# Attention with a borrowed PSUM bank for the row maxima, and the burst of products with v moved to the end of its head step

## The chip, the core and the metric

The kernel runs on one core of one Trainium2 chip. The core's engines are TensorE (PE, matrix products; its weight loads are listed apart as PEld), VectorE (DVE), ScalarE (ACT), GpSimd (POOL) and SyncE (SP, which issues most of the DMAs). Each engine works through its own queue in order. Products are written to PSUM, eight banks of 128 partitions by 512 float32 numbers; DVE and ACT read them there. The metric is the device time of one execution in microseconds, as the median of several runs; one more execution was profiled, and all rows of the trace come from that one.

## The reference

Two independent computations are laid side by side. The second is a spectral filter, a 2-D real FFT of a 2048 x 576 array, a product with complex weights, and the inverse transform. The change does not touch it. The first, cut to what matters here:

```python
B, S, D = 1, 2048, 576;  H = 32; Dh = 18; N = 4; L = 512
q, k, v = x @ wq, x @ wk, x @ wv              # split into 32 heads and 4 segments
for s in range(N):
    logits = q_s @ k_s^T * scale + mask       # causal within the segment
    p = softmax(logits);  a_dot = p @ v_s
    pq = phi(q_s);  a_mem = (pq @ M) / (pq @ z + 1e-6)
    o = g * a_mem + (1 - g) * a_dot           # g = sigmoid(beta) by head
    M += phi(k_s)^T @ v_s;  z += sum(phi(k_s))
out = o @ wo
```

So there are 4 segments x 32 heads = 128 score matrices of 512 x 512, of which the lower triangle counts. The softmax subtracts the maximum of each row.

## The kernel before

The program runs in stages: the forward FFT with the loads of weights, the projections to q, k and v, the inverse FFT with the first maxima, and then the attention, which is where the change lies. q, k and v are stored in DRAM and read back in stacks of 8 heads (`Qs`, `Ks`, and `vs` for v). A stack's rows 0 to 107 carry three-way bfloat16 splits of the 18 values of a head; rows 108 and 109 of `Qs` hold the row maxima, so that the second product of scores comes out with the maxima already subtracted.

**The loop.** `attention` loops over head steps t = 0 to 132, one head per step; four heads (a quad, k = t // 4, hh = t % 4) share a tile. The order is written out by hand: the order in which the source issues instructions is that of each engine's queue. One step interleaves several lines of work, most of them Python generators that `steps` advances:

- `s1(t+11)` is the first pass for the head eleven steps ahead. It forms the scores in parts, two for an even head, three for an odd one (the third part holds a block of each head of the pair). Each `part` takes a PSUM bank `s1`, of which the pool `ps1` has three, makes one or two products on PE (L687), each of 128 to 512 columns, and has DVE add the mask and take the row maxima (L691) into `mg`. As t+11 is odd when t is even, the step with three parts has even t.
- `s2(t)` is the second pass: scores transposed (L723, L727 and L728, in odd steps also L733 for the pair), and exp on ACT (L724, L729, L734) into the tiles `P`. I call these three tiles p0, p1 and p2. They have three banks, tag `s2`. After the fourth head of a quad POOL clears the upper triangle (`sel`, L736); the rest of the selections come one step later (`s.rest`).
- `pv` is the product of P with v (L760), float32, four heads side by side in 32-column strips of the array. It comes in bursts of eight calls, which the trace shows as 16 products with as many weight loads, at odd t: t % 4 = 1 opens the bank `pv` of the quad before, t % 4 = 3 completes it, and `pv_out` copies it to `U` on ACT (from t = 117 on, on DVE). From there it goes to DRAM (`u_dmas`).
- `mpath(k+2)` carries the maxima of a quad from columns to rows: POOL casts (L703, L704), in the next step (hh = 1) PE transposes (L707, into a bank `s1`), ACT copies (L710), and two steps later ACT issues the DMA into rows 108 and 109 of `Qs` (L713).
- The background list `bg`, advanced by `run_bg` at a rate of 1.0 to 1.35 calls a step, holds the set-up of the output weights, the denominators of the memory part (`den`, L811), the mixing of memory and attention (`mixed`, with `combine` L884 and `mem1` L835 and L841) and the output projection of the segment before (`oproj`, L908). Its products take the one bank `post`, through the function `post`; from t = 117 on they take `s1` banks, as the maxima are then all done. `late_setup`, the first entry, takes no bank.
- `lane` holds the chains of reciprocals (`recip`, L785 and L786 on DVE).

PSUM during the loop: `s1` three banks, `s2` three, `pv` one, `post` one.

Within one step the order is: first part of the maxima, p0, background left over, second part, p1, the burst (odd t), background, third part (even t), transposition (t % 4 = 1), p2 (odd t), the copy of the transposition.

After the loop the last output projection runs (`last_proj`, L937), with small products (L917) between.

Of the kernel before, what the change touches and what calls it, by code (L numbers as in the profile page):

```python
# [5 lines left out]
F32=mybir.dt.float32; F32R=mybir.dt.float32r  # L6
# [403 lines left out]
class ATT:  # L410
# [268 lines left out]
    def s1(s,t):  # L679

        nc=s.nc; k,hh=divmod(t,4); n,qd=divmod(k,2); h=4*qd+hh
        Q,K=s.Qs[n%3],s.Ks[n%4]; tp=s.sm
        assert (n,0) in s.loaded and (n,1) in s.loaded,(t,n)
        if hh==0: s.mg[k]=tp.tile([128,4,4],F32,name="mg")
        def part(*J):
            p=s.ps1.tile([128,512],F32,name="s1",tag="s1")
            for o,i,e in J: nc.tensor.matmul(p[:,o:o+128*i+128],Q[:108,h+e,128*i:128*i+128],K[:108,h+e,:128*(i+1)],start=True,stop=True)  # L687
            for o,i,e in J:
                w=128*(i+1); b=max(256,w-128*e)
                junk=tp.tile([128,b],BF,name=f"junk{b}",bufs=1)  # L690
                nc.vector.tensor_tensor_reduce(out=junk[:,:w],in0=p[:,o:o+w],in1=s.mask[:,512-w:],scale=1.0,scalar=-3.0e38,  # L691
                    op0=OP.add,op1=OP.max,accum_out=s.mg[k][:,hh+e,i:i+1])
        part((0,2,0),(384,0,0))
        yield
        part((0,3,0))
        yield
        if hh%2: part((0,1,-1),(256,1,0))
        yield
# [247 lines left out]
    def begin(s,sm,sp,ps1):  # L946
        s.late=[]; s.now=-1
        s.sm,s.sp,s.ps1=sm,sp,ps1
        s.mh=sm.tile([128,8,16],BF,name="mh",bufs=1); s.nc.gpsimd.memset(s.mh,0.0)
        s.mg={};s.P={};s.vs={};s.rc={};s.am={};s.pq={};s.ux={};s.rate=1.2;s.potag=s.rest=None  # L950
    def prologue(s):

        nc,io=s.nc,s.io
        yield
        s.load_v(0)
        q=s.stack_dmas(1,0)+s.stack_dmas(1,1)+s.stack_dmas(2,0)+s.stack_dmas(2,1)+[lambda: s.load_v(1)]+s.stack_dmas(3,1)
        for i in range(2): yield
        i=0
        for t in range(11):
            for _ in s.s1(t):  # L960
                for _ in range(1+(i%24==0)):
                    if q: q.pop(0)()
                i+=1
                yield
            if 2<=t<6: nc.gpsimd.dma_start(s.Ks[t-2][108:110].rearrange("p h c -> p (h c)"),io["neg1"])
            if t in (3,7): m=s.mpath(t//4); next(m)
            if t in (4,8): next(m); next(m,None)
        assert not q
# [3 lines left out]
    def attention(s,tp,ps):  # L972
        nc=s.nc; s.tp,s.ps,s.psm,s.mtag=tp,ps,s.ps1,"s1"
        s.homes()
        def steps(gen,i):
            for _ in range(i):
                try: next(gen)
                except StopIteration: return
        m=None
        q=[]  # L980
        qu=[]
        bg=[s.late_setup(tp)]
        state=dict(acc=0.0)
        def run_bg(rate):
            state["acc"]+=rate
            if state["acc"]>=1:
                state["acc"]-=1
                while bg:
                    try: next(bg[0]); break
                    except StopIteration: bg.pop(0)  # L990
        lane=[]
        for t in range(133):
            k,hh=divmod(t,4); n,qd=divmod(k,2); g=k//8
            if hh==0 and qd==0:
                if 0<n<14: q+=s.stack_dmas(n+2,0)
                if 0<n<13: q+=s.stack_dmas(n+3,1)
                if n+2<16: q.insert(6,lambda n=n: s.load_v(n+2))
            st=t%32
            if t in (18,21,24,27,30): s.pq_load(1,ORD[(18,21,24,27,30).index(t)])
            if t==34: bg.append(s.den(1,lane))  # L1000
            if st==8 and g>0:
                def ln(g=g):
                    r=s.recip(s.rD[g-1],s.rrD[g-1],s.g1,False,"rr",2)
                    for i in range(8):
                        if 2<i<6: s.ux_load(g-1,ORD[i-3])
                        next(r); yield
                    yield from r
                    bg.append(s.mixed(g))
                    o=s.oproj(g-1)
                    if g<3: bg.append(itertools.islice(o,4)); bg.append(s.den(g+1,lane))  # L1010
                    bg.append(o)
                lane.append(ln())
            if t==125: lane.append(s.recip(s.rD[3],s.rrD[3],s.g1,False,"rr"))
            a=s.s1(t+11) if t+11<128 else iter(())
            b=s.s2(t) if t<128 else iter(())
            for _ in range(3 if t%8==0 else 1):
                if q: q.pop(0)()
            if qu: qu.pop(0)()
            steps(a,1)
            steps(b,1)  # L1020
            run_bg(0)
            steps(a,1)
            steps(b,1)
            if 4<=t-1<132: s.pv((t-5)//4,(t-5)%4)
            run_bg(s.rate)
            steps(a,1)
            if hh==1 and m is not None: steps(m,1)
            steps(b,1)
            if hh==1 and m is not None: steps(m,1)
            if hh==0 and k+2<32: m=s.mpath(k+2); next(m)  # L1030
            if hh==0 and s.rest: s.rest(); s.rest=None
            if t>=7 and t%4==3:
                s.pv_out((t-7)//4)
                if t%8==3:
                    u=s.u_dmas((t-11)//8)
                    if t<124: s.later(1,lambda u=u: qu.extend(u))
                    else: qu+=u
            for l in list(lane):
                try: next(l)
                except StopIteration: lane.remove(l)  # L1040
            if qu: qu.pop(0)()
            s.due(t)
        assert not q
        s.potag="s2"; s.last_parts()
        if qu: qu.pop(0)()
        b=s.recip(s.rD[3],s.rrD[0],s.g1,False,"rd"); next(b)
        for u in range(3): s.ux_load(3,u)
        while qu: qu.pop(0)()
        i=0
        while bg or i<10:  # L1050
            for l in list(lane):
                try: next(l)
                except StopIteration: lane.remove(l)
            run_bg(1.0)
            i+=1
            s.due(132+i)
            if i in (3,8,10): s.last_tile((3,8,10).index(i),"rr")
            if i==3: s.ux_load(3,3)
            if i==5: next(b); next(b); next(b)
            if i in (6,7): next(b)  # L1060
            if i==7: s.ux_load(3,4)
        assert not lane
        s.due(999)
        for _ in b: pass
        s.last_low()
        for t in range(3):
            for u in range(7):
                s.last_proj(u,t)
                if t==2 and u==3: s.last_low()
                if t==2 and u in (1,4): s.last_tile(3 if u==1 else 4,"rd")  # L1070
        s.last_low()
        for u in range(7): s.last_proj(u,3)
        o=[s.tp.tile([128,4,512],F32,name=f"P{i}").rearrange("p a b -> p (a b)") for i in range(2)]
        o=[o[tb//3][:,576*(tb%3):576*(tb%3)+576] for tb in range(4)]
        nc=s.nc
        for u in range(8):
            if u==6:
                for t in range(4): s.last_proj(7,t)
            tb,hf=divmod(u,2); s.last_proj(u,4); c=slice(288*hf,288*hf+288) if u>5 else slice(0,576)
            (nc.vector.tensor_copy if hf else nc.scalar.copy)(o[tb][:,288*hf:288*hf+288],s.acc[u])  # L1080
            if hf or u>5: nc.sync.dma_start(s.io["ya"][1536+128*tb:1664+128*tb,c],o[tb][:,c])
# [108 lines left out]
```

## Time and profile before

| | |
|---|---|
| median of 3 runs | 684.14 us (683.86 to 684.6) |
| profiled execution | 683.95 us |
| its span, first to last instruction | 682.2 us |
| mean granted TensorE clock | 0.999 |
| instructions | 14101 |
| first product of the second pass (L723) | at 347.6 us |
| last product of the first pass (L687) | at 617.9 us |
| last burst of products with v (L760) | at 645.0 us |

How to read the rows: a row of the timeline has the start in us, the time it took, the engine, the line, the operation, what it writes <- what it reads, the partitions and elements, how many instructions are merged into it, and in brackets the idle time of the engine before it and what ended it. A matmul's end is modelled and includes its way through the array, so two that follow each other overlap in the rows; the distance of their starts is what PE spends on one. A row of the chain that ended last has start, length, engine, tile, line and count. A row of a table of windows has the window, its length, and the busy time of PE, PEld, DVE, ACT and POOL with the number of instructions, then clock, DMA share and GB/s; where the view was asked for one engine it has only that one. A row of a line's group has the count, the durations in ns (least, median, most) and the first and the last start.

### The profile page before, as it was taken

To read this page: it belongs to the slowest core of one execution; us is meant where nothing else is said; L and a number is where in the kernel's file an instruction comes from. 1 tells how busy PE (TensorE), PEld (TensorE's weight loads), DVE (VectorE), ACT (ScalarE), POOL (GpSimd) and SP (SyncE) were. 2 spreads that over 40 slices of the span, in tenths; PEclk is the share of its full clock that TensorE was granted. 3 is DMA by queue.
4 is the path that set the end of the run, shared out by engine and by line. 5 is a ranking of instruction groups with operands and counts; after the bars stand their busy time and mean duration, and the time that the engine had idled before them with its cause. 6 is when DMAs were issued, how large, how long until landed. Compare 5 with 4: busy or idle time off the path is not lost.

```text
span 682.2 us, 14101 instructions
## 1 busy us (share of the span) xinstructions
PE 669.0 (98%) x4776; PEld 487.0 (71%) x4776; DVE 541.0 (79%) x1509; ACT 433.5 (64%) x900; POOL 193.0 (28%) x392
## 2 busy tenths in 40 slices
PE   9999999999999999999989999999999999999997
PEld 5999779879879879999954444444566445663497
DVE  5998989889789779598778888998766888667543
ACT  4876795585585384544358877777756777656521
POOL 2111000100200102556416433445323663135410
PEclk9999999999999999999999999999999999999999
DMA  9896476596387679699336765776646576423152
GB/s 338 301 311 186 137 198 200 151 300 203 113 240 222 178 211 319 196 284 272 110 121 176 207 185 151 204 205 174 173 139 188 155 186 167 125 87 92 29 170 78
DMA packets 76034, 127.57 MB, mean 187 GB/s; under 512 B 12813, under 2 KB 44203, under 8 KB 72371
## 3 DMA queue, kind: packets, MB, share of 16 engines
q1 hardware_dynamic: 69310, 110.67, 55.7%
q0 software_dynamic: 5632, 15.76, 8.0%
q8 instruction: 37, 0.61, 0.4%
q10 hardware_dynamic: 1020, 0.25, 0.2%
q14 instruction: 35, 0.28, 0.1%
HBM read 81.78 MB, written 43.92 MB: 184 GB/s over the span
## 4 chain that ended last, share of the span: by engine, by line
PE 84%; DVE 5%; DMA 4%; ACT 3%; issue 2%; POOL 1%; SPq 0%; ACTq 0%; DVEq 0%; POOLq 0%
PE pj L487 15%; PE pv L760 11%; PE s L687 11%; PE pjv L487 8%; PE po L908 5%; PE i L331 4%; PE i L320 4%; PE f L145 4%; PE c L166 4%; PE s L723 3%; PE s L727 3%; PE pn L835 2%; PE s L733 2%; PE po L937 2%; PE pm L559 2%
## 5 line engine op out<-in xcount | busy, mean ns | idle before, releaser
L691 DVE CUSTOM_DVE_ANT_0 junk<-s,x 128x384 bf16<-128x384 f32 (+3 forms) x512 | 219.6, 486 | 49.0 <-PE s L687 47.6
L736 POOL TENSOR_SCALAR_AFFINE_SELECT P<-P 128x512 f32<-128x512 f32 (+2 forms) x135 | 80.3, 617 | 61.3 <-ACT P L724 58.0
L760 PE MATMUL pv<-P,vs 128*32 128x512 f32 (+3 forms) x1024 | 82.2, 439 | 0.5 <-POOL P L736 0.4
L724 ACT ACTIVATE P<-s 128x512 f32<-128x512 f32 x128 | 77.3, 604 | 8.3 <-PE s L723 7.1
L729 ACT ACTIVATE P<-s 128x512 f32<-128x512 f32 x128 | 77.0, 602 | 2.8 <-PE s L728 2.7
L734 ACT ACTIVATE P<-s 128x512 f32<-128x512 f32 x64 | 38.3, 598 | 46.3 <-PE s L733 45.4
L687 PE MATMUL s<-Ks,Qs 108*128 108x512 bf16 (+3 forms) x256 | 57.9, 299 | 2.2 <-DVE mg L691 2.0
L760 PEld LDWEIGHTS pv<-P,vs 128*32 128x32 f32 x1024 | 26.8, 109 | 45.5 <-issue 36.3
L487 PE MATMUL pj<-x,wqkh 128*128 128x512 f32 x162 | 56.1, 408 | 0.0
L232 DVE TENSOR_TENSOR Z<-Z 128x580 f32<-128x580 f32 (+2 forms) x51 | 45.9, 913 | 0.6
L691 DVE DVE_READ_ACCUMULATOR2_ANT mg<- 128x1 f32 x512 | 42.5, 83 | 0.0
L548 POOL MEMSET vt<- 128x32 f32 x16 | 2.3, 162 | 139.2 <-PE pm L559 79.2
L320 PE MATMUL i<-civ,Y 128*128 128x256 f32 (+1 forms) x288 | 39.6, 289 | 0.9 <-POOL Y L305 0.9
L687 PEld LDWEIGHTS <-Qs 108*128 108x128 bf16 x320 | 29.5, 97 | 13.0 <-issue 6.2
L320 PEld LDWEIGHTS i<-civ,Y 128*128 128x128 f32 (+1 forms) x288 | 36.8, 181 | 1.9 <-POOL Y L305 1.3
L331 PE MATMUL i<-itab,T 128*128 128x290 f32 (+1 forms) x224 | 36.0, 304 | 0.1
L487 PE MATMUL pj<-x,wqkl 128*128 128x512 f32 x90 | 35.5, 395 | 0.0
L487 PE MATMUL pj<-xh,wqkh 128*128 128x512 f32 x90 | 35.5, 395 | 0.0
L487 PE MATMUL pj<-xh,wqkl 128*128 128x512 f32 x90 | 35.5, 395 | 0.0
L487 PEld LDWEIGHTS pj<-x,wqkh 128*128 128x128 f32 x162 | 30.5, 189 | 6.4
L506 DVE SCALAR_TENSOR_TENSOR ex<-pj,ex 128x512 f32<-128x512 f32 (+1 forms) x28 | 19.3, 689 | 19.4 <-ACT ex L504 19.4
L500 ACT CAST sp<-pj 128x512 bf16<-128x512 f32 x36 | 21.3, 591 | 18.1 <-PE pj L487 14.4
(207 smaller groups left out, 1697.2 us busy)
## 6 DMA issues: line engine op xcount, KB each, us to landing
qkD<-sp SPq DMA_DIRECT2D x32, 384.0 KB
xin<-xb SPq DMA_DIRECT2D x16, 384.0 KB
cfw<-cfw POOLq DMA_DIRECT2D x16, 384.0 KB, 5.1
civ<-civ POOLq DMA_DIRECT2D x16, 384.0 KB, 7.7
Ks<-qkD SPq DMA_DIRECT2D x12, 512.0 KB
x<-qkD SPq DMA_DIRECT2D x10, 512.0 KB
Qs<-qkD SPq DMA_DIRECT2D x10, 512.0 KB
vs<-vD SPq DMA_DIRECT2D x16, 310.5 KB
```

The lines of the kernel that those rows point to most:

```text
L232: s.nc.vector.tensor_tensor(o,a,b,op=op)
L320: nc.tensor.matmul(p[:m,k],Y[i][:,q,c*128:c*128+m],cc[:,hl,o:o+256],start=n==0,stop=n==5)
L331: nc.tensor.matmul(p,x,t,start=n==0,stop=n==6)
L487: s.nc.tensor.matmul(out,a,b,start=i==0,stop=i==len(L)-1)
L687: for o,i,e in J: nc.tensor.matmul(p[:,o:o+128*i+128],Q[:108,h+e,128*i:128*i+128],K[:108,h+e,:128*(i+1)],start=True,stop=True)
L691: nc.vector.tensor_tensor_reduce(out=junk[:,:w],in0=p[:,o:o+w],in1=s.mask[:,512-w:],scale=1.0,scalar=-3.0e38, op0=OP.add,op1=OP.max,accum_ ...
L724: nc.scalar.activation(P[0][:,hh],p0,AF.Exp,scale=SC)
L729: nc.scalar.activation(P[1][:,hh],p1,AF.Exp,scale=SC)
L734: nc.scalar.activation(P[2][:,hh-1:hh+1].rearrange("p h c -> p (h c)"),p2,AF.Exp,scale=SC)
L736: nc.gpsimd.affine_select(out=x[:,a:b],in_=x[:,a:b],pattern=[[0,b-a],[1,128]],compare_op=OP.is_ge,fill=0.0,base=0,channel_multiplier=-1)
L760: nc.tensor.matmul(s.pvt[32*hh:32*hh+32,128*j:],vt[:,152*j+19*h:152*j+19*h+32],mv[0][:,hh,mv[1]],start=j==0,stop=j>1,skip_group_check=True)
L908: nc.tensor.matmul(ps,a[t][:r,c],b[:r,t,w],start=i==0,stop=i==13)
```

## The change

Two things change.

First, `part` counts the parts (`s.n1`, from the first part of the inverse FFT's stage on), and while `s.spare` is set every fourth part takes the bank `post` in place of one of the three `s1` banks. `s.spare` is set at the top of each step: for t < 34, and later when the list `bg` is empty.

Second, within a head step the burst of products with v moves from behind p1 to the end, behind the background call, the third part and p2; and the two steps of the transposition, which lay on either side of p2, both follow the burst.

```diff
         def part(*J):
-            p=s.ps1.tile([128,512],F32,name="s1",tag="s1")
+            s.n1+=1
+            p=s.ps.tile([128,512],F32,name="s1",tag="post") if s.spare and s.n1%4==0 else s.ps1.tile([128,512],F32,name="s1",tag="s1")
...
-        s.mg={};s.P={};s.vs={};s.rc={};s.am={};s.pq={};s.ux={};s.rate=1.2;s.potag=s.rest=None
+        s.mg={};s.P={};s.vs={};s.rc={};s.am={};s.pq={};s.ux={};s.rate=1.2;s.potag=s.rest=None; s.n1=0; s.spare=False
...
         for t in range(133):
+            s.spare=t<34 or not bg
             k,hh=divmod(t,4); n,qd=divmod(k,2); g=k//8
...
             steps(a,1)
             steps(b,1)
-            if 4<=t-1<132: s.pv((t-5)//4,(t-5)%4)
             run_bg(s.rate)
             steps(a,1)
-            if hh==1 and m is not None: steps(m,1)
             steps(b,1)
-            if hh==1 and m is not None: steps(m,1)
+            if 4<=t-1<132: s.pv((t-5)//4,(t-5)%4)
+            if hh==1 and m is not None: steps(m,2)
             if hh==0 and k+2<32: m=s.mpath(k+2); next(m)
```

## The prediction

> **What bounds the kernel now.** I read first the page's shares, then the starts of the products with v along the chain that ended last, and then one pair of head steps on PE and on DVE.
>
> ```profile
> span 682.2 us, 14101 instructions
> PE 669.0 (98%) x4776; PEld 487.0 (71%) x4776; DVE 541.0 (79%) x1509; ACT 433.5 (64%) x900; POOL 193.0 (28%) x392
> ```
> ```profile
> 384.27 1.21 PE pv L760 x16
> 388.10 1.22 PE pv L760 x16
> 392.00 1.21 PE pv L760 x16
> ```
>
> PE looks full, but the ends of its matmuls are modelled, so I read its pace from the starts. A burst of products with v comes in every second head step, at odd t from 5 on. Where there is no background the pace is 3.83 us a pair of steps (384.27 to 388.10), then 3.90 (392.00), the longer one with a transposition in it. PE inside the first:
>
> ```profile
> 386.08 0.38 PE L687 MATMUL s<-Ks,x 108*128 108x512 bf16 x1
> 386.30 0.33 PE L727 MATMUL s<-Qs,Ks 110*128 110x384 bf16 x1
> 386.47 0.22 PE L728 MATMUL s<-Qs,Ks 110*128 110x128 bf16 x1
> 386.52 0.38 PE L687 MATMUL s<-Ks,x 108*128 108x256 bf16 x2
> 386.89 0.38 PE L687 MATMUL s<-x,Qs 108*128 108x384 bf16 x2
> 387.11 0.38 PE L723 MATMUL s<-Qs,Ks 110*128 110x512 bf16 x1
> 387.51 0.38 PE L687 MATMUL s<-x,Qs 108*128 108x512 bf16 x1
> 387.72 0.33 PE L727 MATMUL s<-Qs,Ks 110*128 110x384 bf16 x1
> 388.03 1.28 PE L760 MATMUL pv<-P,vs 128*32 128x512 f32 x16
> ```
>
> 512 columns take 0.22 us (386.08 to 386.30). The two products of 256 columns from 386.52 are thus through at 386.74, but the next starts at 386.89: **0.15 us of waiting**. From 387.11 one expects 387.33 and sees 387.51: **0.18 us**. Both late starts are products for the maxima, which need one of three banks. DVE shows for what they wait:
>
> ```profile
> 386.06 0.56 DVE L691 CUSTOM_DVE_ANT_0 junk<-s,x 128x384 bf16<-128x384 f32 x1 [0.46 <-PE s L687]
> 386.76 0.08 DVE L691 DVE_READ_ACCUMULATOR2_ANT mg<- 128x1 f32 x1
> 386.76 0.69 DVE L691 CUSTOM_DVE_ANT_0 junk<-s,x 128x512 bf16<-128x512 f32 x1
> 387.37 0.08 DVE L691 DVE_READ_ACCUMULATOR2_ANT mg<- 128x1 f32 x1
> ```
>
> DVE is through with the first part (384 and 128 columns) at 386.84 and with the second (512) at 387.45; PE goes on 0.05 and 0.06 later. So PE waits for DVE within the pair, and behind the burst DVE waits for PE (0.46 idle). Neither is the bound alone: three banks tie them together.
>
> **The extra bank.** Every fourth part goes to the post bank, while t<34 or the background list is empty. With a part in four elsewhere, the three other banks come round so that each part follows the part four before it, not three. Call the parts of a pair e1 e2 e3 o1 o2: o1 waited for e1, o2 for e2. Now o1 needs the o2 of the pair before, long read, and o2 needs e1, read at 386.84, where o2 would start at about 387.3 without waits. Both waits go: 0.33 us a pair. I take it for the pair of 3.90 too, though no row above shows its inside. The transposition keeps taking one of the three banks, so that one or two parts behind it still have only two or three before them; these come behind the burst, in which DVE reads on. That cover makes it nothing; without it the 0.33 comes back in every second pair. Late next are PE's own 3.50 and 3.57 us a pair, or DVE. The windows show DVE's busy time in the two stretches where the bank is lent, and the groups of lines when the background uses it first and next:
>
> ```profile
> 357.12:411.22 54.10, 47.66 (x228) 1.00 0.69 183
> 419.95:448.36 28.41, 25.39 (x116) 1.00 0.69 191
> ```
> ```profile
> L811 PE MATMUL pd<-pq,zst x24: 592/605/617, 413.7 to 582.2; 126*32 126x512 f32 x24
> L884 PE MATMUL pb<-rr,sel x15: 379/407/430, 449.6 to 626.7; 96*126 96x512 bf16 x12, 96*72 96x512 bf16 x3
> ```
>
> First stretch (burst of t=5 to burst of t=33): 54.10 us are 14 pairs of 3.864. Less 14 x 0.33 = **4.6** it is 49.5; DVE's 47.66 fit in. The steps before t=5 have no burst and DVE paces them; one more bank lets PE run ahead by one part (0.61 for 512 columns, 386.76 to 387.37), so 0 to 0.6; I take 0.2, since a transposition within these steps ties PE to DVE again.
>
> Second stretch: the three calls of the denominators' background at t=34 to 36 are over by t=37, and the next user starts at 449.6 (t=51), so 14 steps, 28.41 us, 7 pairs. The same 0.33 gives 2.3. In it DVE makes reciprocals between the maxima:
>
> ```profile
> 431.85 0.95 DVE L786 RECIPROCAL ry<-ry 128x128 f32<-128x128 f32 x1
> 433.96 0.95 DVE L786 RECIPROCAL ry<-ry 128x128 f32<-128x128 f32 x1
> 435.60 0.38 PE L687 MATMUL s<-Ks,Qs 108*128 108x384 bf16 x2 [1.12 <-DVE mg L691]
> ```
>
> They cost PE 1.12 us (435.60) behind the second one. DVE's 25.39 is the floor, so at most 3.0 can go. PE without any waits would need 28.41 - 2.3 - 1.1 = 25.0, below the floor: the reciprocals' wait mostly stays, since DVE has only 3.5 - 3.3 = 0.2 a pair to catch up. I take **2.5**. In t=82 to 84 and 113 to 116, between two groups of background, I see no step in which the list is sure to be empty: 0.
>
> **The burst behind p2 and the background.** In an odd step PE now goes: maxima, scores p0 and p1, the step's background, p2, burst, transposition. The moved burst is 16 products with as many weight loads; it issues nothing on ACT, POOL, SP or DVE. The transposition is one product and one load; its copy stays on ACT behind p2's exp, and the DMA that ACT issues two steps later keeps its step. POOL's selections keep their order; those of a step's P are wanted two steps later. PE's work is the same and the engine takes it in order, so by itself the move gives nothing in steps in which PE never waits. Three places can change:
>
> ACT: the scores have three banks, so p2 takes the one of the third before it, the p1 of the even step. It now comes right behind this step's p1 and no longer a burst later. The rows of ACT:
>
> ```profile
> 385.84 0.60 ACT L734 ACTIVATE P<-s 128x512 f32<-128x512 f32 x1 [0.94 <-PE s L733]
> 386.34 0.58 ACT L766 COPY U<-pv 128x512 f32<-128x512 f32 x1
> 386.80 0.62 ACT L724 ACTIVATE P<-s 128x512 f32<-128x512 f32 x1
> 387.29 0.62 ACT L729 ACTIVATE P<-s 128x512 f32<-128x512 f32 x1
> ```
>
> That p1's product is the one of 386.30, and its exp ends at 387.91. p2 would want its bank at 387.94 - 0.33 = 387.61 in the new pace, 0.3 too early. But this lag comes from p2's exp at 385.84 and the copy of U queued ahead; with p2 in front of the burst its exp (0.50 to the next, 385.84 to 386.34) is done within the burst, and the lag falls to 387.41. So 0, with 0.36 a pair if the lag stays. U's copy waits for the burst's end at either place, and is the first of ACT's queue then.
>
> The Trainium skill's page "PSUM — Partial Sum Buffer" (Engine vs sequencer instructions) has ScalarE's queue as a strict FIFO; by that rule a copy of U that waits for a late burst holds up every exp behind it. The rows above agree: U started only behind p2's exp, at 386.34, though its burst had ended by 385.5 (384.27 and 1.21).
>
> Background: one bank serves it. From a product in an even step to the next in an odd step there was a burst; now this cover lies between odd and even.
>
> ```profile
> 640.10 0.43 PE L841 MATMUL pb<-rd,sel 96*126 96x512 bf16 x1
> 640.57 0.69 DVE L842 TENSOR_TENSOR am<-am,pb 126x512 f32<-126x512 f32 x1 [1.32 <-PE pb L841]
> ```
>
> Such a bank is free 1.16 us after its product starts (640.10 to 641.26) if DVE is idle, 1.77 with one part of the maxima ahead. The way on PE is 0.22 for the product, 0.22 for e3 and about 0.96 for the next step's maxima and scores (386.89 to 388.03 less 0.18), together 1.40: a wait of 0 to 0.4. Of the 20 products L884 and L841 before t=117 half lie in even steps: 0 to 4 us lost. Against that DVE gets the odd steps' products before the burst, not 1.2 us later, in which it idled (1.32 above), and the odd-to-even way gets the burst as cover. I take 0, with -4 and +2.5 as ends.
>
> End of the loop:
>
> ```profile
> 619.33 1.28 PE L760 MATMUL pv<-P,vs 128*32 128x512 f32 x16 [0.45 <-POOL P L736]
> 621.60 0.23 PE L707 MATMUL mt<-idb,mh 128*128 128x128 bf16 x1 [0.63 <-POOL mh L704]
> 643.92 0.80 PE L908 MATMUL po<-woh,oh 126*128 126x288 f32 x4 [0.68 <-DVE am L837]
> 645.04 1.28 PE L760 MATMUL pv<-P,vs 128*32 128x384 f32 x16
> 646.26 0.40 PE L908 MATMUL po<-wol,oh 126*128 126x288 f32 x1
> ```
>
> At 619.33 the burst waits 0.45 for POOL, and the transposition behind it 0.63. Now the background's product and p2 (0.22 each) fill the first wait instead of coming later: **0.4** gained. Near 643.92 PE waits 0.68; the product two steps earlier is issued 1.2 us sooner, while DVE's reciprocal stays in front of its copy: 0.3 gained. The last burst (645.04) now follows the seven products that begin at 646.26: 0.9 later against these (7 x 0.13). Its output is copied, stored and loaded again, while PE has products back to back (19.32 us busy of 20 in the next row):
>
> ```profile
> 640.00:660.00 20.00, 19.32 (x149) 16.03 (x146) 9.96 (x15) 5.24 (x13) 3.80 (x9) 1.00 0.30 85
> ```
>
> That is the cover: PE's sum is the same and the time stays. If the chain through the DMAs took over, up to 0.9 is lost. I take 0 for the last burst and +0.3 for the other.
>
> **Sum:** 4.6 + 0.2 + 2.5 + 0.4 + 0.3 = 8.0 us. The profiled run took 683.95, its span 682.2, so 675.95; the median of the runs is 0.19 above the profiled one: 684.14 - 8.0 = **676.1**.
>
> **Rivals.**
> 1. *The transposition spoils the rotation.* The wait returns in every second pair: 21 pairs / 2 x 0.33 = 3.5 less gain, 679.6. For it: the transposition is no part and is not counted, so the first parts behind it find the distance of three again. Against: the burst, 1.2 us, lies in between, time for two parts of DVE. 13%.
> 2. *The burst's new place gives more.* DVE's and ACT's idle times in the steps with background go too: the +2.5 above and the reciprocals' other 0.5 make 673.1. For it: 1.32 us of idle DVE before a row like 640.57. Against: there PE has more products per pair and waits little. 12%.
> 3. *ACT becomes the bound.* Its lag stays, p2 waits 0.36 in each of the 21 quiet pairs: 7.6 of 8.0 gone, 683.7, no change. For it: ACT starts p0's exp only at 386.80. Against: 0.94 us idle at 385.84, which the move fills. 6%.
> 4. *Slower: the background's bank in odd steps.* Each of 10 products that follow an even step's product waits with PE until DVE has read that one, behind two parts of maxima (1.16 + 2 x 0.61 = 2.38, less 1.40: 1.0 each), and the burst behind it is late by as much; 10 us, so 686.1. It outweighs the gain from 0.8 us each. Against: DVE can't be two parts behind where it just had a burst's time to drain. 7%.
>
> **How the numbers follow.** 62% is left for the forecast, whose own range is 675.2 to 678.0 (0.5 more to DVE's floor and 0.4 more at the start on one side; 0.09 us of waits left in each of 21 pairs on the other). Less than 0.2% (1.4 us) can't be told from no change here. Faster: 62 + 13 + 12 = 87%; within 0.2%: 6%; slower: 7%. The range takes in rivals 1 and 2 with half a microsecond to spare: 672.5 to 680.5.
>
> **What would show it.** Right: bursts 3.50 to 3.57 us apart in the first stretch, with DVE busy 96% there (47.66 of 49.5) and no gap before a product for the maxima; the burst of t=33 about 4.8 us earlier; 26 us for the second stretch; p2's exp begun while the burst runs; the stretches with background as long as now. Wrong: pairs still above 3.7 us (rotation or ACT, told apart by whether the late product is one for the maxima or p2); PE waiting for DVE's L842 or L889 before an odd step's product (rival 4); a longer end behind the last burst.

## The result and the profile after

The changed kernel takes **676.08 us** (median of 4 runs, 675.3 to 677.27) against 684.21 us before (4 runs, 683.86 to 684.6): a ratio of 0.9883, 95% interval 0.9865 to 0.99, that is 8.1 us less. The prediction was 676.1. The profiled run took 676.22 us. From here on lines of the changed kernel from L687 on have a number one higher than before (the maxima's product L687 is L688, the burst L760 is L761). The page of the changed kernel:

```profile
span 674.5 us, 14143 instructions
PE 660.6 (98%) x4776; PEld 482.9 (72%) x4776; DVE 540.5 (80%) x1509; ACT 443.2 (66%) x900; POOL 194.1 (29%) x392
```

Busy times hardly tell the two kernels apart; the starts of the bursts do. The chain that ended last, changed kernel, first stretch:

```profile
381.87 1.21 PE pv L761 x16
385.38 1.21 PE pv L761 x16
388.94 1.21 PE pv L761 x16
```

The pairs are 3.51 and 3.56 us, where they were 3.83 and 3.90. To see where the rest went I cut the loop at the starts of the bursts of t = 5, 33, 37, 49, 51, 113 and 131 (the last). The windows between them, PE alone, first before. The row of the first stretch is in the prediction, and t=33 to 37 takes 8.73 in both kernels:

```profile
419.95:444.46 24.51, 23.31 (x197) 1.00 0.65 177
444.46:448.36 3.90, 3.89 (x36) 1.00 0.97 279
448.36:610.06 161.70, 161.29 (x1298) 1.00 0.58 160
610.06:645.04 34.98, 32.42 (x253) 1.00 0.21 59
```

and after:

```profile
357.00:406.54 49.54, 49.54 (x456) 1.00 0.78 209
415.27:437.87 22.60, 21.55 (x197) 1.00 0.72 196
437.87:442.64 4.77, 4.25 (x36) 1.00 1.02 289
442.64:604.62 161.98, 161.08 (x1303) 1.00 0.59 158
604.62:637.99 33.37, 31.62 (x251) 1.00 0.22 62
```

First stretch 54.10 to 49.54, second (t=37 to 51) 28.41 to 27.37, background 161.70 to 161.98, end 34.98 to 33.37. One caution in reading the windows: what now comes ahead of the burst lies on the other side of the mark. That is p2 (two products of 256 columns, 0.22) at every mark but t=131, whose step has no p2; at t=51 also one product of 512 columns (0.22); and at t=113 and t=131 a half of the output projection (seven products, 7 x 0.13 = 0.92; from the first of them to the next other product 1.02, so the two gains that use it are good to 0.1). With that taken out, the gains are 0.34 at the start (357.12 to 357.00, and 0.22), 4.56, 1.26 (1.04 + 0.22), 0.42 in the background (0.92 - 0.22 - 0.28), 1.39 at the end (1.61 - 0.22), and -0.27 behind it (37.16 to 36.51 in the marks, less the 0.92): together the 7.7 us between the spans. I call these the gains like for like. In the eight profiles with the change's order at the end the part behind the last burst lies between 35.8 and 37.4 us, so its 0.27 is no finding, and two spans may differ by a microsecond with nothing changed in the loop.

The inside of a pair with a transposition, on PE of the changed kernel, answers to the rows of the prediction:

```profile
379.45 0.23 PE L708 MATMUL mt<-idb,mh 128*128 128x128 bf16 x1
379.51 0.38 PE L688 MATMUL s<-Ks,x 108*128 108x384 bf16 x2
380.34 0.22 PE L729 MATMUL s<-Qs,Ks 110*128 110x128 bf16 x1
380.39 0.60 PE L688 MATMUL s<-Ks,x 108*128 108x256 bf16 x4
380.83 0.38 PE L724 MATMUL s<-Qs,Ks 110*128 110x512 bf16 x1
381.05 0.38 PE L688 MATMUL s<-Ks,x 108*128 108x512 bf16 x1
381.27 0.33 PE L728 MATMUL s<-Qs,Ks 110*128 110x384 bf16 x1
```

The four products from 380.39 (two of 256 columns for the third part of one step, then 384 and 128 for the first of the next) take 0.44 and the next starts at 380.83; the part of 381.05 starts 0.22 behind the scores of 380.83 and the next follows after 0.22. Neither wait of 0.15 or 0.18 is left. By the Trainium skill, "Perfetto Trace Analysis" (Matmuls), independent groups of products should go round through different banks, so that reading one overlaps the next group's products; the run with the bank alone, below, agrees, with pairs of 3.58 us where they were 3.83.

DVE has become nearly full there, as this window of DVE shows:

```profile
357.00:406.54 49.54, 47.73 (x230) 1.00 0.78 209
```

That is 96%. And ACT: the groups of p2's exp on the two pages, before and after.

```profile
L734 ACT ACTIVATE P<-s 128x512 f32<-128x512 f32 x64 | 38.3, 598 | 46.3 <-PE s L733 45.4
```
```profile
L735 ACT ACTIVATE P<-s 128x512 f32<-128x512 f32 x64 | 38.6, 604 | 4.0 <-PE s L734 2.6
```

ACT sat idle 46.3 us before these 64 instructions and now 4.0: p2 comes ahead of the burst, and 60 of the 64 exps begin while the burst runs, where only one did before. One of them, in the burst of 381.87:

```profile
382.29 0.60 ACT L735 ACTIVATE P<-s 128x512 f32<-128x512 f32 x1
```

Four places where PE still waits (timeline of PE, and one row of the chain, changed kernel):

```profile
430.05 0.38 PE L688 MATMUL s<-Ks,Qs 108*128 108x512 bf16 x1 [0.90 <-DVE mg L692]
442.11 0.38 PE L885 MATMUL pb<-rr,sel 96*72 96x512 bf16 x1 [0.50 <-DMA rr<-rrD]
534.70 0.38 PE L842 MATMUL pb<-rd,sel 96*72 96x512 bf16 x1 [0.77 <-ACT am L838]
612.42 0.38 PE L885 MATMUL pb<-rr,sel 96*126 96x512 bf16 x1 [0.55 <-DVE ux L890]
```
```profile
437.25 4.83 DMA rr<-rrD
```

The first is behind the reciprocals, as before. The second is new: the first product of the mixing at t=51 needs the reciprocals from DRAM, whose load was issued at 437.25 and landed 4.83 us later. Before, this product stood behind the burst (449.6, in the prediction's rows) and did not wait. The last two are new as well. They are products of the background in odd steps that wait for the one bank of the background: at 534.70 ACT has not yet copied the product before, at 612.42 DVE has not yet read the one of the even step, having maxima in front. The second is the sign that the prediction named for its rival 4. Smaller waits for DVE of this kind, 0.17 by the starts of the products, come six times between t=51 and t=113 (446.33, 455.19, 460.21, 529.12, 538.92 and 543.94).

### The profile page after: what moved, and what is told of

The parts are those of the page before. It is cut to its first block, busy times and chain, and to the rows that moved or that the text cites. A ratio compares the mean times of both kernels' runs of the same rounds, so it can differ in the third digit from the quotient of the medians.

```text
span 674.5 us, 14143 instructions
## 1 busy us (share of the span) xinstructions
PE 660.6 (98%) x4776; PEld 482.9 (72%) x4776; DVE 540.5 (80%) x1509; ACT 443.2 (66%) x900; POOL 194.1 (29%) x392
## 4 chain that ended last, share of the span: by engine, by line
PE 83%; DMA 5%; DVE 4%; ACT 3%; issue 2%; POOL 2%; SPq 1%; ACTq 0%; POOLq 0%; DVEq 0%
PE pj L487 15%; PE pv L761 10%; PE s L688 10%; PE pjv L487 7%; PE po L909 6%; PE i L331 4%; PE i L320 4%; PE f L145 4%; PE c L166 4%; PE s L724 3%; PE s L728 3%; PE po L938 2%; PE s L734 2%; PE pm L559 2%; PE pn L836 2%
## 5 line engine op out<-in xcount | busy, mean ns | idle before, releaser
L692 DVE CUSTOM_DVE_ANT_0 junk<-s,x 128x384 bf16<-128x384 f32 (+3 forms) x512 | 219.1, 487 | 45.3 <-PE s L688 43.1
L761 PE MATMUL pv<-P,vs 128*32 128x512 f32 (+3 forms) x1024 | 82.2, 439 | 0.0
L761 PEld LDWEIGHTS pv<-P,vs 128*32 128x32 f32 x1024 | 26.8, 109 | 45.4 <-issue 36.8
L688 PE MATMUL s<-Ks,Qs 108*128 108x512 bf16 (+3 forms) x256 | 57.5, 300 | 1.1 <-DVE mg L692 1.1
L692 DVE DVE_READ_ACCUMULATOR2_ANT mg<- 128x1 f32 x512 | 42.6, 83 | 0.0
L688 PEld LDWEIGHTS <-Qs 108*128 108x128 bf16 x320 | 26.9, 98 | 15.5 <-issue 11.2
```

The costliest lines, as they stand in the source:

```text
L761: nc.tensor.matmul(s.pvt[32*hh:32*hh+32,128*j:],vt[:,152*j+19*h:152*j+19*h+32],mv[0][:,hh,mv[1]],start=j==0,stop=j>1,skip_group_check=True)
```

## The experiments

All stretches are from the starts of the bursts, in us; "ratio" is to the kernel before on the same chip, with its 95% interval.

| run | median | ratio | t=5 to 33 | 33 to 37 | 37 to 49 | 49 to 51 | 51 to 113 | 113 to 131 |
|---|---|---|---|---|---|---|---|---|
| before | 684.21 | | 54.10 | 8.73 | 24.51 | 3.90 | 161.70 | 34.98 |
| change | 676.08 | 0.9883 | 49.54 | 8.73 | 22.60 | 4.77 | 161.98 | 33.37 |
| bank only | 678.88 | 0.9928 (0.9913 to 0.9943) | 50.91 | 8.72 | 22.94 | 3.89 | 161.76 | 34.98 |
| move only | 682.78 | 0.9982 (0.9973 to 0.9991) | 54.07 | 8.72 | 24.51 | 4.11 | 161.99 | 33.37 |
| background behind the burst | 678.31 | 0.9918 (0.9903 to 0.9933) | 49.54 | 8.72 | 22.60 | 3.89 | 163.34 | 34.27 |
| first stretch only | 676.45 | 0.9897 (0.988 to 0.9913) | 49.54 | 8.73 | 24.50 | 4.27 | 161.96 | 33.35 |
| short reciprocals | 676.71 | 0.989 (0.985 to 0.993) | 49.54 | 8.73 | 21.63 | 4.18 | 161.95 | 32.89 |
| bank lent in the background | 695.36 | 1.0163 (1.0125 to 1.02) | 49.55 | 8.94 | 22.60 | 5.05 | 179.41 | 34.33 |
| copy on VectorE | 678.74 | 0.9924 (0.9909 to 0.9938) | 50.36 | 8.72 | 22.94 | 3.90 | 162.19 | 34.85 |
| order by stage | 676.26 | 0.9885 (0.9869 to 0.9902) | 49.54 | 8.94 | 22.60 | 3.89 | 162.94 | 33.35 |
| covered load | 675.60 | 0.9883 (0.9867 to 0.99) | 49.54 | 8.73 | 22.60 | 3.89 | 162.58 | 33.36 |
| change again | 675.77 | 0.9885 (0.987 to 0.9899) | 49.54 | 8.73 | 22.60 | 4.69 | 161.98 | 33.37 |

All stretches of the change and of the change again agree to 0.01 us but for 49 to 51, where a load is waited for (4.77 and 4.69). So the table resolves much smaller differences than the medians. The runs are spread over several chips, so medians of different rows are compared by their ratios.

**Bank only: the bank is lent, the order stays as before.**

```diff
(against the changed kernel)
             steps(b,1)
+            if 4<=t-1<132: s.pv((t-5)//4,(t-5)%4)
             run_bg(s.rate)
             steps(a,1)
+            if hh==1 and m is not None: steps(m,1)
             steps(b,1)
-            if 4<=t-1<132: s.pv((t-5)//4,(t-5)%4)
-            if hh==1 and m is not None: steps(m,2)
+            if hh==1 and m is not None: steps(m,1)
```

> The bank is lent as in the change; the burst, the transposition and the background stay in the order of before. My theory, that the bank alone carries the gain of the quiet stretches: bursts 3.51 and 3.57 us apart in the first stretch, the burst of t=33 about 4.7 us earlier than before, the second stretch a little shorter than in the change (no product of the background has to come ahead of the burst of t=51), about 26.5 us; from there to the end as before; in all 6 to 6.8 us faster, 677.4 to 678.2. Rival, that the scores p2 ahead of the burst are needed for it (ACT's lag): pairs stay above 3.6 us and the gain is under 5 us.

My theory fell in part: 678.88 is above its range, and the first stretch takes 50.91, so the bank alone gives 3.19 of the 4.56. The gain, 4.9 us, is just under the rival's 5, but its pairs above 3.6 are four only: those without a transposition take 3.58, three of those with one 3.57. What holds back the rest is mostly ACT, in two places. PE and ACT of this run:

```profile
376.82 0.60 ACT L735 ACTIVATE P<-s 128x512 f32<-128x512 f32 x1 [0.22 <-PE s L734]
377.31 0.58 ACT L767 COPY U<-pv 128x512 f32<-128x512 f32 x1
377.78 0.61 ACT L725 ACTIVATE P<-s 128x512 f32<-128x512 f32 x1
378.44 0.32 PE L728 MATMUL s<-Qs,Ks 110*128 110x384 bf16 x1
...
379.97 0.23 PE L708 MATMUL mt<-idb,mh 128*128 128x128 bf16 x1
380.58 0.60 ACT L735 ACTIVATE P<-s 128x512 f32<-128x512 f32 x1
381.07 0.24 ACT L711 COPY mts<-mt 32x128 bf16<-32x128 bf16 x1
381.36 0.60 PE L688 MATMUL s<-Ks,x 108*128 108x256 bf16 x4
```

Behind the burst ACT has p2's exp and the copy of U in a row, so p0's exp begins at 377.78 and ends at 378.39; p1 of the next step wants p0's bank and starts at 378.44, 0.075 later than PE could. And the transposition of 379.97 has its copy only at 381.07, because p2's exp stands ahead of it on ACT. The bank comes free at 381.31 and the next part that takes it starts at 381.36, 0.23 late. Over the 14 pairs PE loses 1.37 us: 0.08 in each of the seven pairs without a transposition, and 0.16 to 0.25 in four of the seven with one. Three of these four are such copies; in the first pair (t=5) the transposition itself came 0.2 late, behind POOL's cast of the maxima. In the changed kernel p2's product lies ahead of the burst, its exp begins earlier, and the copy ends 0.52 us after the start of the transposition in five of the seven pairs that have one, where it took 1.22 to 1.34 with the bank alone. The slowest case is this one, as a cast of the set-up (L652) stands in front on ACT:

```profile
378.79 0.67 ACT L652 CAST wol<-ob 32x576 fp32r<-32x576 f32 x1
379.48 0.60 ACT L735 ACTIVATE P<-s 128x512 f32<-128x512 f32 x1
379.98 0.24 ACT L711 COPY mts<-mt 32x128 bf16<-32x128 bf16 x1
```

The transposition is at 379.45 there, so the bank is back 0.77 after it (380.22); in the rows of the bank alone it took 1.34.

**Move only: the order is the change's, no bank is lent.**

```diff
-            s.n1+=1
-            p=s.ps.tile([128,512],F32,name="s1",tag="post") if s.spare and s.n1%4==0 else s.ps1.tile([128,512],F32,name="s1",tag="s1")
+            p=s.ps1.tile([128,512],F32,name="s1",tag="s1")
...
-            s.spare=t<34 or not bg
```

> The burst and the transposition are moved as in the change; no bank is lent. My theory: nothing in the two quiet stretches (3.83 and 3.90 us a pair as before), a loss of about 0.3 to 1 us between t=51 and t=113, since the background's products now wait in odd steps, and a gain of 2 to 2.5 us from t=113 to the end: 682.0 to 683.2. Rival, that the end came sooner only because the stretches before it did (loads already there): no gain at the end, 684 to 685.

The windows of this run, PE alone:

```profile
357.60:411.67 54.07, 53.86 (x457) 1.00 0.71 193
611.00:644.37 33.37, 31.61 (x251) 1.00 0.22 62
```

In the quiet stretches the move alone gives nothing (54.07 against 54.10, 24.51 both): with three banks PE waits for DVE, and it doesn't matter that ACT is earlier. The end is as short as in the change, 33.37, while with the bank alone it stays 34.98. So the gain at the end, 1.61 us at the marks and 1.39 like for like, belongs to the move and not to the bank; I had expected 2 to 2.5. The time, 682.78, lies in my range. The two parts are not additive at the start (3.19 and 0.03 alone, 4.56 together) and independent at the end.

**The transposition's copy on VectorE**, otherwise bank only:

```diff
-        nc.scalar.copy(mt,pt[:32])
+        (nc.scalar.copy if s.now<0 else nc.vector.tensor_copy)(mt,pt[:32])
```

> The bank alone is lent, burst and transposition as before (as e1_bank_only), but in the loop the copy of the transposed maxima is made by VectorE and not by ScalarE. My theory, that with the bank alone the first stretch still lost 1.4 us to ScalarE: about 0.8 because the transposition's bank is freed by its copy, which stood behind p2's exp, and 0.55 as the scores p1 wait 0.08 us in every second pair for an exp. Here the first part goes and the second stays: pairs with a transposition 3.57 each time and not 3.73 to 3.82, the first stretch 0.7 to 0.9 us shorter than with the bank alone. Rival, that the bank's rotation itself is spoilt behind a transposition: the pairs of 3.7 to 3.8 stay.

DVE and ACT of this run, with the transposition at 365.13:

```profile
365.49 0.21 DVE L711 COPY mts<-mt 32x128 bf16<-32x128 bf16 x1
365.67 0.60 ACT L735 ACTIVATE P<-s 128x512 f32<-128x512 f32 x1
```

The copy no longer stands behind the exp, which comes later, and the pairs with a transposition fall to 3.57, but for the first (3.79, POOL's cast) and one of 3.66, whose 0.09 I did not follow; the first stretch takes 50.36, 0.55 less than with the bank alone. The seven waits of 0.08 for p0's bank stay, as they should. So of the 1.37 the transposition's copy costs 0.55, which this run shows; 7 x 0.075 is put down to p0's exp by the rows alone, 0.22 is the first pair, and 0.09 stays open. It is no gain over bank only in the time (678.74 and 678.88).

**First stretch only: the bank is lent for t < 34 and never later.**

```diff
-            s.spare=t<34 or not bg
+            s.spare=t<34
```

> As the change, but the bank is lent for t<34 alone. My theory: the second stretch gets its waits of 0.33 a pair back, and a little less for the pair with the reciprocals, which the fourth bank hardly shortened: 1.7 to 2.2 us slower than the change, 677.8 to 678.3. Rival, that DVE is the bound in the second stretch whatever the banks: under 0.7 us slower, 676.8 at most.

From t=37 to 51 it takes 28.77 us (24.50 and 4.27) against 27.37 in the change and 28.41 before. So the bank gives 1.90 in the six pairs to t=49, and in the seventh it loses 0.50 again: what is early there waits for the load. So the 1.7 to 2.2 us that I expected are gained and mostly lost again inside the stretch. The time lies where the rival had it, but not for its reason: DVE was not the bound in the six pairs. The medians differ by less than the stretches do, 676.45 and 676.08; the part behind the last burst happened to be the shortest of all here (35.8).

**Short reciprocals.** Only 16 of 128 columns are inverted; the rest of the denominators is left as it is, so this kernel doesn't compute the softmax and is no version to use.

```diff
-        nc.vector.reciprocal(y,y)
+        nc.vector.reciprocal(y[:,:16],y[:,:16])
```

> As the change, but each reciprocal works on 16 of its 128 columns, so that the rest of the sums goes on without being inverted and the output is another. My theory, that the two reciprocals of 0.95 us on VectorE make the wait that the fourth bank couldn't take away in the second stretch: the pair of the burst of t=43, 4.88 us in the change, falls to about 3.6, the second stretch is 1.1 to 1.4 us shorter, and the end about 0.4 shorter, since a reciprocal also stands before a copy there: 1.5 to 2 us faster than the change in all. Rival, that VectorE's own work on the maxima is the bound of that stretch with four banks: the pair stays above 4.3.

The reciprocals in the changed kernel and in this one, rows of DVE:

```profile
426.30 0.95 DVE L787 RECIPROCAL ry<-ry 128x128 f32<-128x128 f32 x1
428.41 0.95 DVE L787 RECIPROCAL ry<-ry 128x128 f32<-128x128 f32 x1
```
```profile
425.92 0.25 DVE L787 RECIPROCAL ry<-ry 128x16 f32<-128x16 f32 x1
427.33 0.25 DVE L787 RECIPROCAL ry<-ry 128x16 f32<-128x16 f32 x1
```

The pair of t=43 falls from 4.88 to 3.91 us, and with it 37 to 49 from 22.60 to 21.63. The wait of 0.90 behind the second reciprocal is theirs, then. The pair is still 0.34 above its neighbours (3.57), not at the 3.6 that I expected, and I did not follow that. In this run 49 to 51 is shorter too, by 0.59, and the end by 0.48. The median of two runs (674.61 and 678.80) says nothing on the time.

**Background behind the burst: p2, burst, background, transposition in odd steps.**

```diff
+            if t%2: steps(b,1)
+            if 4<=t-1<132: s.pv((t-5)//4,(t-5)%4)
             run_bg(s.rate)
             steps(a,1)
-            steps(b,1)
-            if 4<=t-1<132: s.pv((t-5)//4,(t-5)%4)
+            if t%2==0: steps(b,1)
```

> As the change, but in odd steps the background's call comes behind the burst: maxima, p0, p1, p2, burst, background, transposition. My theory, that the background ahead of the burst loses its cover in odd steps (the changed kernel waits 0.66 us for a load at t=51, 0.93 for a bank near 530 us, and about 0.16 eight times): these waits go, and what the end gained by filling its waits goes in part: second stretch about 0.7 shorter; t=51 to t=113 about 1.5 shorter; from t=113 to the end 1 to 2 longer; in all between 675 and 677. Rival, that these waits are paid for elsewhere by the engines that cause them: the stretch from t=51 to t=113 stays within 0.5 us of the changed kernel's.

The load's wait is gone (49 to 51 takes 3.89, as before), but my theory of a shorter stretch with background fell: it takes 163.34, 1.64 longer than before, and the end gains only 0.71 (0.49 like for like). The time, 678.31, is above my range. PE and DVE of this run just behind t=51:

```profile
443.61 0.68 DVE L888 TENSOR_TENSOR am<-ux,pb 72x512 f32<-72x512 f32 x1 [0.47 <-PE pb L885]
444.22 0.55 DVE L692 CUSTOM_DVE_ANT_0 junk<-s,x 128x384 bf16<-128x384 f32 x1
444.56 0.38 PE L688 MATMUL s<-Ks,Qs 108*128 108x256 bf16 x2
445.04 0.38 PE L688 MATMUL s<-x,Qs 108*128 108x384 bf16 x2
```

DVE's sum for the background now stands in its queue at 443.61, ahead of the maxima of the next step, in which DVE would catch up; the maxima begin at 444.22, and the part at 445.04 comes 0.26 late (444.56 and 0.22 is 444.78). A product of the background ahead of the burst lets DVE do that sum during the burst. That the whole 1.64 is made of such places I did not add up.

**Bank lent in the background too**, for t < 67, 82 to 98 and from 114.

```diff
-            s.spare=t<34 or not bg
+            s.spare=t<67 or 82<=t<99 or t>=114
```

> As the change, but the bank is lent for t<67, for 82 to 98 and from 114 on, so also in steps whose background products of one call want it. Rival 4 of the prediction, stretched to its full size: products of the background and parts of the maxima now wait for one another on one bank. My theory: the waits of 0.1 to 0.5 us a pair for the three banks go in 16 pairs, but the background's products wait for VectorE nearly as much: within 1 us of the change from t=51 to t=113. Should contention be strong: over 3 us longer there.

Slower, 1.0163: t=51 to 113 takes 179.41, 17.4 more than in the change, and the growth starts with the first products of the mixing. PE of this run, and then a window over most of t=51 to 113:

```profile
445.06 0.38 PE L885 MATMUL pb<-rr,sel 96*72 96x512 bf16 x1 [1.10 <-DVE mg L692]
...
462.71 2.07 PE L836 MATMUL pn<-pq,Mst 126*126 126x512 f32 x2 [1.39 <-DVE mg L692]
```
```profile
443.00:604.00 161.00, 145.72 (x1142) 0.98 0.54 149
```

My theory of at most 1 us fell. Here the background's product waits for DVE to read a part of the maxima (releaser L692) in the bank both use. That is a wait like rival 4's, at more than 1 us a time in these rows, but not the same: rival 4 had a product of the background in the bank, not a part of the maxima. In the change the bank is lent only while the list is empty. Not all of the 17.4 need be waits: the granted clock was 0.98 over these 161 us, which makes an estimate of up to 3 us (2% of 161).

**Order by stage**: bank lent for t < 51, 82 and 114; in odd steps p2, burst, background for t < 52, the order of before to t = 112, the change's after that.

```diff
-            s.spare=t<34 or not bg
+            s.spare=t<51 or t in (82,114)
...
+            o=0 if t<52 else 1 if t<113 else 2
...
```

> Put together from the stretches of the runs so far: the bank lent for t<51 and at t=82 and 114; the order with the background behind the burst and p2 ahead of it for t<52, the order of before from t=52 to 112, the order of the change from t=113. My theory, that the stretches add up: from the burst of t=5 to the end about 1 us shorter than the change, 9 to 9.5 us shorter than before, 674.6 to 675.2. Rival, that a stretch made shorter only lets the next one wait for loads and sums that are timed by steps: no faster than the change, 676 or more.

No faster than the change (676.26 and 676.08), as the rival said. It has 3.89 in 49 to 51, but lending the bank at t=35 and 36, where the denominators use it, costs 0.21 net (8.94 against 8.73), and 51 to 113 takes 162.94; without the 0.92 of the projection's half that is 162.02, against 161.70 before.

**Covered load: the change, with the background behind the burst in odd steps for t < 52**, and on the same chip **the change again**.

```diff
+            o=t<52 and t%2
+            if o:
+                steps(b,1)
+                if t>4: s.pv((t-5)//4,(t-5)%4)
             run_bg(s.rate)
             steps(a,1)
-            steps(b,1)
-            if 4<=t-1<132: s.pv((t-5)//4,(t-5)%4)
+            if not o:
+                steps(b,1)
+                if 4<=t-1<132: s.pv((t-5)//4,(t-5)%4)
```

> The change, with one difference: for t below 52 the background work of an odd step is emitted behind the burst again (p2's product, burst, background, transposition of the maxima); from t=53 on, and at the end, everything is as in the change, and so is the lending of the bank. Theory: in the changed kernel the product L885 of t=51 waits 0.66 us for the load of the reciprocals, which was issued at 437.25 and took 4.83 us; behind the burst it has the burst's length more time, so this wait goes. Then, counted from the burst of t=5, the burst of t=51 comes about 0.9 us earlier than in the change (0.66 of the wait and 0.22 of the product that now stands behind the burst), the first stretch is unchanged (4.56 us shorter than before), and some 0.4 to 0.7 us are left at the end: about 675.5 us, ratio to the kernel before about 0.9875. Rival: it is given back later, as the gain at t=51 of the run with the order by stage was at t=113, and the time is the change's, 676 us.

> The changed kernel once more, without an edit, so that the run with the covered load is compared on the same chip. Theory and rival alike: about 676 us, 0.988 of the kernel before; burst of t=33 4.56 us and burst of t=51 5.6 us earlier than before, counted from the burst of t=5; the wait of L885 at t=51 for the load of the reciprocals is there again, 0.5 to 0.7 us. If the wait is absent here, it belonged to one execution, and the run with the covered load can gain nothing by it.

The wait was there again in the change (0.42 of idle before L885 on PE, where the first profile had 0.50):

```profile
442.48 0.38 PE L885 MATMUL pb<-rr,sel 96*72 96x512 bf16 x1 [0.42 <-DMA rr<-rrD]
```

and is gone with the load covered:

```profile
443.00 0.41 PE L885 MATMUL pb<-rr,sel 96*72 96x512 bf16 x1
```

The pair falls from 4.69 to 3.89, but the next stretch takes 0.60 more (162.58 against 161.98). Of both, 0.22 is the product itself, which now lies behind the mark. So 0.58 of waiting is won and 0.38 lost again; behind the burst of t=51 a part of the maxima is late by the same 0.26 as in the run with the background behind the burst, with DVE's sum ahead of it again. The 0.20 that is left in the trace can't be seen in the times, 675.60 and 675.77. The time lies within what theory and rival both allow; in the trace most of the gain is given back, as the rival said.

No version of these beats the change by more than the runs vary.

## Why the prediction was right, and where its steps were not

The time was right, 676.1 against 676.08, and the way it came about mostly so. That it agrees to 0.1 us is luck: errors of opposite sign in the terms cancelled, and single runs of the changed kernel lie between 675.3 and 677.27.

1. **First stretch, 4.6: measured 4.56, but not by the bank alone.** Pairs of 3.50 to 3.57, no wait before a part, DVE at 96%, all as said. The step that failed is the one that credits the lent bank with all of 14 x 0.33. The bank alone gives 3.19. The sentence that "by itself the move gives nothing in steps in which PE never waits" holds for the run with the move alone (0.03), but it was read as if PE would not wait in the old order once the bank was lent. It does wait there, mostly for ACT: the transposition's bank, which I had watched for its place in the rotation, is late because ACT's copy of it queues behind p2's exp, and p1's bank because p0's exp queues behind p2's exp and the copy of U. The run with the copy on VectorE shows the first; the second rests on the rows. The move takes away both, and the late transposition of the first pair: 1.37 us. The prediction had named the ACT lag of p2 and rightly said that the move shrinks it; it had not asked what the lag would cost without the move, nor looked at the copy's place in ACT's queue.
2. **Start, 0.2: 0.12 at the mark, 0.34 like for like**, both less than the start of the loop differs from run to run (355.98 to 359.45 over the profiles).
3. **Second stretch, 2.5: measured 1.04 at the mark, 1.26 like for like.** Six of the seven pairs gave 1.91, 0.32 each, as reckoned. The pair with the reciprocals is one of them: 0.29 came off it, and their own wait stayed, as reckoned. The extra 0.2 did not come. What failed is the seventh pair, which is 0.87 longer instead of 0.33 shorter: at t=50 the list already holds the mixing, so no bank is lent in it ("14 steps" was one too many); one product of 0.22 now stands ahead of the mark; and its product waits 0.66 for a load, by the starts of the products. The step "Background: ... I take 0" had asked only when the bank comes free, not whether the product's own data would be there a burst earlier.
4. **Background, 0 (-4 to +2.5): 0.42 gained like for like.** The waits that the step reckoned with, 0 to 0.4 for each of ten products, did come in part: six of 0.17 for DVE and, by the starts, one of 0.93 for ACT (534.70); a seventh for DVE, 0.71, falls behind t=113 (612.42). What outweighed them I did not add up. Rival 4 had the right mechanism, at 1.0 each a size that was not reached.
5. **End, 0.7: measured 1.61 at the marks, 1.39 like for like**, and by the move alone (33.37 in both runs with it, 34.98 without). Mechanism half as said. The output projection's product waits 0.19 instead of 0.68, as said, and 0.49 instead of the 0.3. The 0.4 for the burst did not come in the way said: the burst no longer waits 0.45 for POOL, but the background's product now ahead of it waits 0.55 for DVE (612.42). In its place the transposition, which the sum left out, waits 0.35 instead of 0.63. These rows of the changed kernel answer to the prediction's:

```profile
614.58 0.23 PE L708 MATMUL mt<-idb,mh 128*128 128x128 bf16 x1 [0.35 <-POOL mh L705]
635.95 0.79 PE L909 MATMUL po<-woh,oh 126*128 126x288 f32 x4 [0.19 <-DVE am L838]
```

   I had priced the end by such idle times, and they start at the modelled end of the product before, so they are too short. The windows show it: PE's idle time from t=113 to 131 falls by 0.81 (34.98 - 32.42 to 33.37 - 31.62), while the stretch is 1.39 shorter like for like. Where the rest lies I did not add up.
6. **Last burst behind the output projection, 0: right.** The time behind it, with the moved products counted, differs by 0.27, within the variation of that part.

Against the forecast, point 3 lost 1.24 us, point 6 0.27 and point 1 0.04; points 2, 4 and 5 won 0.14, 0.42 and 0.69. That makes 7.7 between the two profiled spans, and the medians differ by 8.1. Rival 1 (the transposition spoils the rotation) did not show in any of the 14 pairs; rival 2 is true at the end only; rival 3's lag is real, at 0.08 us in seven pairs, in the order of before with the bank lent, and absent in the change.

## What to carry to other kernels

A bank is late for one of two reasons: too few in the rotation, or a reader that has it in its queue behind other work. Here adding a bank showed the second; look, for every bank of the rotation, the odd users too (a transposition), at what stands ahead of its reader. When work is moved earlier past a burst, ask for every operand whether it lands in time, loads included, and not only for the buffer. And cut the trace at marks that recur in both kernels, and count the work between them, since a move can carry some of it past a mark (0.92 us here). Nearly all the stretches agreed to 0.01 us between two executions of the change, where its times scatter by 2 us; but a stretch that is gained need not be kept at the end.

## What the runs showed of the hardware

- Lending the same bank to two producers came with 17.4 us more in a stretch of 162. PE was busy 145.72 of 161 us there, and 161.08 of 161.98 in the change. The granted clock was 0.98 over those 161 us, and 1.00 in the windows of the others, so a part of the 17.4, by the estimate above up to 3 us, may be the clock's.
- The load of 96 KB of reciprocals took 4.83 us (4.75 in the second profile) from issue to landing, behind loads of a stack on SP's queue. By the Trainium skill, "DMA: Bandwidth & Descriptors" (Anatomy of one DMA), a DMA from GpSimd takes some 2.0 us and its bytes at 436 GB/s; that makes an estimate of 2.2 us. The page gives it for another path, and the traces here show over twice that on SP's; that the queue ahead is the cause was not tried.
- A reciprocal of 128 x 128 took 0.95 us and of 128 x 16 0.25 us on DVE, which by a straight line through the two makes 6 ns a column and 0.15 us for the rest (an estimate).
